# Seven block products in another order, with the sums between them, in a mixer kernel's channel stage

## Chip, cores and metric

The program runs on one core of a Trainium2 chip. The metric is device time in microseconds (us) of one execution; the time before is the median of three runs, 832.79 (832.41 to 833.27).

## What is computed

The reference is local attention (8 batches, 8 heads, 576 positions, 64 wide, a window of 64), whose output x (8 x 576 x 512) goes through a mixer:

```python
xt = x.transpose(0, 2, 1)
h = np.maximum(xt @ w_tok1, 0.0) @ w_tok2          # 576 -> 256 -> 576
u = x + h.transpose(0, 2, 1)
h2 = np.maximum(u @ w_ch1, 0.0) @ w_ch2            # 512 -> 1536 -> 512
return (u + h2).astype(np.float32)
```

The last two lines are the channel stage, which the change is about. All is float32. A product is made of three matmuls in the reduced format fp32r on values split in two: hi·hi, hi·lo and lo·hi, where hi is the value rounded by a copy and lo is what the copy left over.

## The kernel before

The program first does attention and the token mixing, and stores u to DRAM in nine chunks of 512 tokens. Then comes the channel stage: three **plain chunks** (numbers 0 to 2), each a first product (`gemm1`, twelve feature tiles `ft`) and a second one (`gemm2`, four output tiles `ct`, in two halves of six feature tiles each for chunks 1 and 2), and then three **pairs** of chunks, (3, 4), (5, 6) and (7, 8).

A pair uses the Winograd form of Strassen's scheme: the two chunks side by side are one matrix of 2 x 2 blocks, and a block product takes seven products, named m1 to m7, in place of eight. The sums of weight blocks that m5, m6, m7 and m3 need are made once, while the plain chunks run, by `weight_steps`: a generator of 24 steps for the first weight ("u") and 24 for the second ("d"), of which a plain chunk takes one or two behind each tile. A step adds weight blocks on VectorE (DVE), and `keep` splits the sum (ScalarE, ACT, copies hi; VectorE subtracts to lo) into buffers `whi` and `wlo`, three each, and stores both to DRAM (`w1s`, `w2s`) through SyncE's queue (SP). `load_unit` brings the weights of one pass back, three passes ahead.

The input sums of a pair (`sums`, `sum4`) and their splits (`prep`) are made beside the pair before, or beside chunk 2 for the first pair.

A pair runs three **groups** (`g`); a group is two **first products** (`first_product`, feature tiles 2g and 2g+1, here pass 1 and pass 2) and two **second products** (`second_product`, ct 0 and ct 1). Each of these four is 42 matmuls: seven products of two tiles of three matmuls. There are nine groups in all.

A first product writes four banks of PSUM, P, Q, R and S, a different four in pass 1 and pass 2, and the second products use the same two sets. m1 goes to P, m6 to Q, m7 to R, m5 to S (k < 4 starts a bank); m2, m3 and m4 are then added into P, S and R (`INTO`), so each of these three waits until the earlier content of its bank has been read. VectorE forms the chain (x1 is a copy of P by ScalarE, then x1 += Q, and so on) and, from the activated sums, the inputs of the second product: `raw_block` and `raw_low` are a block taken from a bank with ReLU and its lo part (VectorE), `sum_block` splits a sum t1 to t4 (hi on ScalarE, lo on GpSimd, POOL). Buffers of these have one copy each per pass.

A second product adds its banks into u2 and into the blocks c11, c12, c21, c22 of the output (`add`, tiles uf). In the last group of a pair (`final`), u2 is added into c12, c21 and c22, and the four blocks are stored. The hooks `last_first`, `last_second0` and `last_second1` put the splits for the next pair between the products of that group.

All engines work in the order in which the program is written here (the schedule is manual), each queue in order.

Of the kernel before, what the change touches and what calls it, by code (L numbers as in the profile page):

```python
# [34 lines left out]
CHUNK = 512  # L35
# [20 lines left out]
PRODUCTS = ("m1", "m6", "m7", "m5", "m2", "m3", "m4")  # L56
# [6 lines left out]
WW = 2 * P  # L63

# [22 lines left out]
def mixer_kernel(ctx: ExitStack, tc: tile.TileContext, qh, kh, vh, wt1, wt2, wc1, wc2, out):  # L87
# [472 lines left out]
    with ExitStack() as bctx:  # L560
# [146 lines left out]
        def weight_steps(name, whi, wlo, part, store, swap):  # L707

            for n in range(2 * NG):
# [17 lines left out]
                nc.vector.tensor_add(s1, s1, a)  # L727
# [3 lines left out]
                if swap:  # L731
                    nc.vector.tensor_sub(a, a, c)
                else:
                    nc.vector.tensor_sub(a, c, a)
                nc.vector.tensor_sub(c, s1, c)
# [45 lines left out]
        def prep(q, m, t, at=0, eng=nc.vector):  # L781
# [4 lines left out]
            split(nc.scalar, eng, c[:, 0, t], c[:, 1, t], raws[at][SOURCE[m]])  # L786
# [3 lines left out]
        for j in range(1, N_PLAIN):  # L790
# [4 lines left out]
            for half in range(2):  # L795
                g = []
                for ft in range(half * NH, (half + 1) * NH):
                    g.append(new_g(f"{j}_{ft}"))
                    gemm1(j, ft, u, g[-1])
                    for _ in range(2 if j == 1 and ft < 8 else 1):  # L800
                        next(steps, None)
# [31 lines left out]
                for ct in range(NCT):  # L833
# [3 lines left out]
                    next(steps, None)  # L837
# [24 lines left out]
        def first_product(n, q, f, after):  # L862
# [18 lines left out]
            def sum_block(m, x):  # L881
                split(nc.scalar, nc.gpsimd, *gc[m, i], x)

            x1, x2, g11, t1, t2, t3, t4 = (tmp("x1", 2), tmp("x2"), tmp("g11"), tmp("g12t"), tmp("g22t"),
                                           tmp("g3"), tmp("g4"))
            for k, m in enumerate(PRODUCTS):
# [7 lines left out]
                if m == "m1":  # L894
                    nc.scalar.copy(x1, pp)  # L895
                elif m == "m6":
                    nc.vector.tensor_add(x1, qq, x1)
                elif m == "m7":
                    nc.vector.tensor_add(x2, rr, x1)  # L899
                elif m == "m5":  # L900
                    nc.vector.tensor_add(qq, ss, x2)  # L901
# [167 lines left out]
```

## Time and profile before

| | |
|---|---|
| median of three runs | 832.79 us |
| the profiled execution | 831.14 us, its span 829.1 us |
| mean granted TensorE clock | 0.997 |
| busy: TensorE, VectorE, ScalarE, GpSimd | 800.3, 603.1, 389.4, 246.4 us |
| pair stage, first to last matmul | 457.05 to 825 us |

The span is what the profiler saw from the first to the last instruction; the profiled execution's own time holds some 2 us around it. A row of the timeline has the start, the length, the engine, the line, the operation, out<-in and, in brackets, how long the engine stood idle before it and what ended that. A row of the stretches has, behind the stretch and its length, the busy time of PE, PEld (weight loads), DVE, ACT and POOL with the number of instructions of each, the granted clock, the DMA share and GB/s. A row of the waits has who waited for whom, the total in us, how often, and the longest. A group's row has the busy time and the mean length of one in ns, then the idle time ahead. Names are the program's with buffer numbers left out: `gp` are the banks of a first product, `op` those of a second, x are x1 and x2, g, g12t and g22t the sums t1 to t4.

### The profile page before, as it was taken

Reading aid. Unit: us, or ns where it says so; the run is one execution under the profiler, and the core shown is the slowest. Engines: PE = TensorE matmul, PEld = TensorE weight load, DVE = VectorE, ACT = ScalarE, POOL = GpSimd, SP = SyncE. Lnnn points to the kernel's source line nnn. Section 1 sums busy time; section 2 is a strip of 40 time slices with the busy share of each in tenths; the row PEclk is TensorE's granted clock in tenths of the full one; section 3 lists DMA queues with packets and bytes.
Section 4 is the critical chain, followed back from the end, with each engine's and each line's share of the span. In section 5 each row is a group of like instructions: output and inputs, shape, how many; then the busy total and the mean of one; then the engine's idle time right before and its main releaser. Section 6 shows DMA issues by size and latency. Waiting matters only on the chain. (4 is left out here: it accounts for less than half of the span.)

```text
span 829.1 us, 15813 instructions
## 1 busy us (share of the span) xinstructions
PE 800.3 (97%) x5749; PEld 654.7 (79%) x5749; DVE 603.1 (73%) x1545; ACT 389.4 (47%) x1124; POOL 246.4 (30%) x225
## 2 busy tenths in 40 slices
PE   8989999999999999999999899999999999999997
PEld 6668888888888878788888677777777877787876
DVE  5978889799773993776858665658766669756566
ACT  7988988988964521232423322244323144324140
POOL 3632544444330000000000122639222648222231
PEclk9999999999999999999999999999999999999999
DMA  9837769677644629956537775755864746855532
GB/s 356 288 140 242 249 233 295 244 225 275 199 130 155 192 78 271 288 176 198 178 113 243 274 286 188 276 182 183 319 234 177 279 179 232 324 185 184 202 141 102
DMA packets 86829, 180.60 MB, mean 218 GB/s; under 512 B 8800, under 2 KB 51808, under 8 KB 84832
## 3 DMA queue, kind: packets, MB, share of 16 engines
q1 hardware_dynamic: 84640, 177.76, 62.3%
q10 hardware_dynamic: 2112, 1.84, 0.7%
q8 instruction: 45, 0.74, 0.4%
q14 instruction: 32, 0.26, 0.1%
HBM read 137.69 MB, written 41.88 MB: 217 GB/s over the span
## 5 line engine op out<-in xcount | busy, mean ns | idle before, releaser
L892 PE MATMUL gp<-m,w1hi 128*128 128x512 f32 x504 | 158.4, 396 | 8.8 <-DVE gp L901 5.6
L108 POOL TENSOR_TENSOR m5lo<-g12t,m5hi 128x512 fp32r<-128x512 f32 x18 | 23.4, 1299 | 418.9 <-ACT m5hi L105 418.9
L892 PEld LDWEIGHTS gp<-m,w1hi 128*128 128x128 f32 x504 | 94.0, 189 | 34.4 <-DVE gp L901 9.4
L301 ACT ACTIVATE e<-e,nm 128x128 f32<-128x128 f32 x288 | 112.2, 397 | 5.9 <-DVE nm L293 5.7
L892 PE MATMUL gp<-m,w1lo 128*128 128x512 f32 x252 | 98.7, 392 | 0.0
L939 DVE TENSOR_TENSOR uf<-op,uf 128x512 f32<-128x512 f32 (+1 forms) x91 | 61.0, 681 | 43.6 <-PE op L949 42.9
L293 DVE CUSTOM_DVE_ANT_0 e<-s,mask 128x128 f32<-128x128 f32 x288 | 65.3, 285 | 9.9 <-PE s L278 9.9
L633 PE MATMUL gp<-ulo,w1hi 128*128 128x512 f32 x144 | 56.0, 389 | 0.0
L633 PE MATMUL gp<-uhi,w1hi 128*128 128x512 f32 x144 | 56.0, 389 | 0.0
L633 PE MATMUL gp<-uhi,w1lo 128*128 128x512 f32 x144 | 56.0, 389 | 0.0
L301 ACT ACTIVATION_READ_ACCUMULATOR e<-e,nm 128x1 f32 x288 | 56.0, 194 | 0.0
L892 PEld LDWEIGHTS gp<-m,w1lo 128*128 128x128 f32 x252 | 47.7, 189 | 10.3
L108 POOL TENSOR_TENSOR xlo<-x,xhi 128x512 fp32r<-128x512 f32 x32 | 41.6, 1301 | 43.5 <-ACT xhi L105 42.8
L641 PE MATMUL op<-ghi,w2hi 128*128 128x512 f32 x128 | 50.0, 390 | 1.0 <-ACT ghi L620 1.0
L641 PE MATMUL op<-glo,w2hi 128*128 128x512 f32 x128 | 50.2, 392 | 0.6 <-DVE glo L621 0.6
L641 PE MATMUL op<-ghi,w2lo 128*128 128x512 f32 x128 | 49.8, 389 | 0.0
L895 ACT COPY x<-gp 128x512 f32<-128x512 f32 x18 | 10.5, 584 | 83.4 <-PE gp L892 83.4
L217 POOL TENSOR_TENSOR w<-r,c 128x384 f32<-128x384 f32 (+1 forms) x28 | 27.6, 986 | 70.2 <-DVE r L215 67.8
L308 PE MATMUL pp<-ident,e 128*128 128x128 f32 x288 | 45.4, 282 | 1.6
L320 PEld LDWEIGHTS xp<-v,pt 128*64 128x64 f32 x1152 | 36.6, 138 | 12.9 <-ACT e L301 9.4
L278 PE MATMUL s<-k,q 64*64 64x128 f32 x1152 | 41.5, 276 | 2.5 <-DVE ri L332 0.9
L416 PE MATMUL up<-t2hi,hhi 128*128 128x320 f32 (+1 forms) x128 | 43.1, 337 | 0.6 <-ACT t2hi L105 0.6
(203 smaller groups left out, 2043.7 us busy)
## 6 DMA issues: line engine op xcount, KB each, us to landing
v<-vh SPq DMA_DIRECT2D x36, 512.0 KB, 4.1
w1hi<-w1s SPq DMA_DIRECT2D x18, 896.0 KB, 4.8
w1lo<-w1s SPq DMA_DIRECT2D x18, 896.0 KB, 6.5
w1hi<-w2s SPq DMA_DIRECT2D x18, 896.0 KB, 4.5
w1lo<-w2s SPq DMA_DIRECT2D x18, 896.0 KB, 6.3
raw<-wc SPq DMA_DIRECT2D x32, 384.0 KB, 4.7
q<-qh SPq DMA_DIRECT2D x36, 256.0 KB, 4.5
k<-kh SPq DMA_DIRECT2D x7, 1280.0 KB, 7.7
```

The costliest lines, as they stand in the source:

```text
L108: eng_lo.tensor_sub(lo, src, hi.bitcast(F32))
L217: (nc.vector if late else nc.gpsimd).tensor_add(w, rf, cf)
L278: nc.tensor.matmul(so, qt[r, j, half], kbs[b][r, n:n + 2, j], start=True, stop=True)
L293: nc.vector.tensor_tensor_reduce(out=e[:, h], in0=s[:, h], in1=mk, scale=-scale, scalar=MAX_F32, op0=ALU.add, op1=ALU.min, accum_out=nm[:, ...
L301: nc.scalar.activation(e[:, h], e[:, h], AF.Exp, bias=nm[:, g:g + 1], scale=-1.0, accum_out=sm[:, g:g + 1])
L308: nc.tensor.transpose(pp[:, h], e[:, h], ident)
L320: nc.tensor.matmul(xp[half * BLK:(half + 1) * BLK, h], pts[h % 2][:, h // 2, half * BLK:(half + 1) * BLK], vt[:, half, h], start=True, sto ...
L416: nc.tensor.matmul(up[:, :n], hx[:, cs], w[:, tt * S + s0:tt * S + s0 + n], start=False, stop=(k == 6), skip_group_check=True)
L633: nc.tensor.matmul(gp, w[:, w1_at(ft, ct)], x[:, ct], start=(k == 0), stop=(k == 3 * NCT - 1))
L641: nc.tensor.matmul(op, w[:, ct, ft], x[:, cols], start=(first and k == 0), stop=(last and k == 3 * len(gs) - 1), skip_group_check=not (fir ...
L892: nc.tensor.matmul(b[INTO[m]], w[:, at], c[:, h, t], start=(k < 4 and z == y == 0), stop=(z == 1 and y == 2), skip_group_check=True)
L939: nc.vector.tensor_add(x, y, x)
```

## The change

It puts the products in another order, in the first products and in the second ones, changes the chain of sums to fit, hands the end of a first product (`tail`: rr, t4 and the m2 and m4 blocks) to the caller, which runs it between the next product's sums (or right behind, after pass 2), takes the weight steps by a table that ends in the first half of chunk 2, lets GpSimd add u2 into the output blocks except in the last pair, and splits the preparation for the next pair into its ScalarE and its GpSimd part. To fit the other signs of the chain, two weight sums of "d" are negated in the same instruction (`negate` in place of `swap`).

```diff
-PRODUCTS = ("m1", "m6", "m7", "m5", "m2", "m3", "m4")
+PRODUCTS = ("m1", "m6", "m5", "m7", "m3", "m2", "m4")
+STEPS_FT = {1: (2, 2, 2, 2, 1, 0, 2, 2, 0, 1, 1, 0), 2: (2, 0, 0, 2, 1, 0, 0, 0, 0, 0, 0, 0)}
+STEPS_CT = {1: (2, 2), 2: (3, 0)}
...
-                    for _ in range(2 if j == 1 and ft < 8 else 1):
+                    for _ in range(STEPS_FT[j][ft]):
                         next(steps, None)
...
-                    next(steps, None)
+                    for _ in range(STEPS_CT[j][half]):
+                        next(steps, None)
...
+            def tail():
+                nc.vector.tensor_add(rr, rr, x1)
+                raw_block("m2", rr)
+                yield
+                positive(t4, rr, t2)
+                sum_block("m4", t4)
+                yield
+                raw_low("m2", rr)
+                yield
...
                 if m == "m1":
                     nc.scalar.copy(x1, pp)
+                    next(earlier, None)
                 elif m == "m6":
                     nc.vector.tensor_add(x1, qq, x1)
+                    next(earlier, None)
+                elif m == "m5":
+                    nc.vector.tensor_add(x2, ss, x1)
+                    next(earlier, None)
                 elif m == "m7":
-                    nc.vector.tensor_add(x2, rr, x1)
-                elif m == "m5":
-                    nc.vector.tensor_add(qq, ss, x2)
+                    nc.vector.tensor_add(qq, rr, x2)
                     raw_block("m3", qq)
-                    raw_low("m3", qq)
-                elif m == "m2":
-                    nc.scalar.activation(g11, pp, AF.Relu)
-                    raw_block("m1", pp)
-                    raw_low("m1", pp)
                 elif m == "m3":
                     nc.vector.tensor_add(ss, ss, x1)
-                    positive(t1, ss, g11)
+                    nc.scalar.activation(g12, ss, AF.Relu)
+                    raw_low("m3", qq)
+                    positive(t3, qq, g12)
+                    sum_block("m7", t3)
+                elif m == "m2":
+                    positive(t1, pp, g12)
                     sum_block("m5", t1)
-                    positive(t2, qq, t1)
+                    nc.vector.scalar_tensor_tensor(out=t2, in0=qq, scalar=0.0, in1=t1, op0=ALU.max, op1=ALU.add)
+                    raw_block("m1", pp)
                     sum_block("m6", t2)
-                    positive(t3, pp, t2)
-                    sum_block("m7", t3)
-                else:
-                    nc.vector.tensor_add(rr, rr, x1)
-                    raw_block("m2", rr)
-                    positive(t4, rr, t2)
-                    raw_low("m2", rr)
-                    sum_block("m4", t4)
+                    raw_low("m1", pp)
...
-        ORDER2 = (("m1", 0), ("m1", 1), ("m6", 0), ("m7", 0), ("m5", 0), ("m5", 1), ("m6", 1), ("m7", 1),
+        ORDER2 = (("m6", 0), ("m7", 0), ("m5", 0), ("m1", 0), ("m1", 1), ("m7", 1), ("m5", 1), ("m6", 1),
                   ("m2", 0), ("m2", 1), ("m3", 0), ("m3", 1), ("m4", 0), ("m4", 1))
...
+            eng2 = nc.vector if q == len(pairs) - 1 else nc.gpsimd
...
-                    if m == "m4" and i == 1:
-                        add(c21[:, cols], bank[:, cols])
...
-                elif m == "m5":
+                elif m in ("m7", "m5"):
                     add(c22, bank)
                 elif m == "m6":
                     add(u2, bank)
                     if final:
-                        add(c22, u2)
-                elif m == "m7":
-                    add(c22, bank)
-                    store(3, c22)
-                    if final:
-                        add(c12, u2)
-                        add(c21, u2)
+                        add(c12, u2, eng2)
+                        add(c21, u2, eng2)
+                        add(c22, u2, eng2)
+                        store(3, c22)
...
             def last_second1(m):
-                if m == "m1":
+                if m == "m5":
                     for t in range(2):
-                        sum4(t, nc.gpsimd)
-                if m in ("m6", "m7"):
+                        sum4(t)
+                if m in ("m1", "m2", "m3"):
                     for t in range(2):
-                        prep(q + 1, {"m6": "m3", "m7": "m4"}[m], t, t)
+                        prep(q + 1, {"m1": "m3", "m2": "m2", "m3": "m4"}[m], t, t, part=0)
+                if m == "m4":
+                    for k in ("m3", "m2", "m4"):
+                        for t in range(2):
+                            prep(q + 1, k, t, t, nc.gpsimd, part=1)
```

On VectorE, between pass 1 and pass 2 of a pair's second group (numbers `_0_2` and `_0_3`: pair 0, feature tiles 2 and 3; `gp0_2_2` is bank R of pass 1), there stood before:

```order
L860 SCALAR_TENSOR_TENSOR g3_0_2_6715<-gp0_2_0_6692,g22t_0_2_6714 128x512
L917 TENSOR_TENSOR gp0_2_2_6694<-gp0_2_2_6694,x1_0_2_6710 128x512
L860 SCALAR_TENSOR_TENSOR g4_0_2_6716<-gp0_2_2_6694,g22t_0_2_6714 128x512
L860 SCALAR_TENSOR_TENSOR m2lo_0_2_6705<-gp0_2_2_6694,m2hi_0_2_6704 128x512
L897 TENSOR_TENSOR x1_0_3_6804<-gp0_3_1_6787,x1_0_3_6804 128x512
L899 TENSOR_TENSOR x2_0_3_6805<-gp0_3_2_6788,x1_0_3_6804 128x512
L901 TENSOR_TENSOR gp0_3_1_6787<-gp0_3_3_6789,x2_0_3_6805 128x512
L860 SCALAR_TENSOR_TENSOR m3lo_0_3_6801<-gp0_3_1_6787,m3hi_0_3_6800 128x512
```

And at the same place now (x2 now reads `gp0_3_3`, bank S):

```order
L871 SCALAR_TENSOR_TENSOR m1lo_0_2_6697<-gp0_2_0_6692,m1hi_0_2_6696 128x512
L899 TENSOR_TENSOR gp0_2_2_6694<-gp0_2_2_6694,x1_0_2_6710 128x512
L920 TENSOR_TENSOR x1_0_3_6798<-gp0_3_1_6781,x1_0_3_6798 128x512
L871 SCALAR_TENSOR_TENSOR t4g_0_2_6716<-gp0_2_2_6694,t2g_0_2_6714 128x512
L923 TENSOR_TENSOR x2_0_3_6799<-gp0_3_3_6783,x1_0_3_6798 128x512
L871 SCALAR_TENSOR_TENSOR m2lo_0_2_6707<-gp0_2_2_6694,m2hi_0_2_6706 128x512
L926 TENSOR_TENSOR gp0_3_1_6781<-gp0_3_2_6782,x2_0_3_6799 128x512
L929 TENSOR_TENSOR gp0_3_3_6783<-gp0_3_3_6783,x1_0_3_6798 128x512
```

The end of pass 1 (rr, t4, m2lo), which stood ahead of pass 2's x1 in one piece, now stands between pass 2's sums.

On GpSimd, at the end of the first pair (`m5_1` is the next pair's input of m5, `uf4` is c12 and c22, `uf3` is c21), there stood before, behind the lo parts of pass 2:

```order
L108 TENSOR_TENSOR m4lo_0_5_7127<-g4_0_5_7134,m4hi_0_5_7126 128x512
L108 TENSOR_TENSOR m7_1_7225<-r12_1_0_6882,m7_1_7225 128x512
L108 TENSOR_TENSOR m7_1_7225<-r12_1_1_6892,m7_1_7225 128x512
L108 TENSOR_TENSOR m5_1_7248<-t1_1_0_6888,m5_1_7248 128x512
L108 TENSOR_TENSOR m5_1_7248<-t1_1_1_6898,m5_1_7248 128x512
L108 TENSOR_TENSOR m2_1_7260<-r21_1_0_6886,m2_1_7260 128x512
L108 TENSOR_TENSOR m2_1_7260<-r21_1_1_6896,m2_1_7260 128x512
L777 TENSOR_TENSOR r11_1_0_6880<-r21_1_0_6886,t2_1_0_6889 128x512
L777 TENSOR_TENSOR r11_1_1_6890<-r21_1_1_6896,t2_1_1_6899 128x512
```

And now:

```order
L112 TENSOR_TENSOR m4lo_0_5_7121<-t4g_0_5_7128,m4hi_0_5_7120 128x512
L796 TENSOR_TENSOR m5_1_7238<-t1_1_0_6888,m5_1_7238 128x512
L796 TENSOR_TENSOR m5_1_7238<-t1_1_1_6898,m5_1_7238 128x512
L959 TENSOR_TENSOR uf4_6480<-u2_0_0_6388,uf4_6480 128x512
L959 TENSOR_TENSOR uf3_6478<-u2_0_0_6388,uf3_6478 128x512
L959 TENSOR_TENSOR uf4_6480<-u2_0_0_6388,uf4_6480 128x512
L796 TENSOR_TENSOR m7_1_7263<-r12_1_0_6882,m7_1_7263 128x512
L796 TENSOR_TENSOR m7_1_7263<-r12_1_1_6892,m7_1_7263 128x512
L959 TENSOR_TENSOR uf4_6480<-u2_0_1_6389,uf4_6480 128x512
L959 TENSOR_TENSOR uf3_6478<-u2_0_1_6389,uf3_6478 128x512
L959 TENSOR_TENSOR uf4_6480<-u2_0_1_6389,uf4_6480 128x512
L796 TENSOR_TENSOR m3_1_7306<-r22_1_0_6884,m3_1_7306 128x512
```

Six additions have come in, `sum4` (r11) has gone to VectorE, and six lo parts (m3, m2 and m4, of which the last row is the first) now stand behind all of them, where there were m2's two ahead of `sum4`.

On VectorE, at the end of chunk 1's first feature half (`glo1_5` is the lo part of the sixth feature tile), there stood before:

```order
L621 SCALAR_TENSOR_TENSOR glo1_4_5256<-gp1_4_5257,ghi1_4_5255 128x512
L715 TENSOR_TENSOR wau_2_5272<-w1hi_66,w1lo_67 128x256
L715 TENSOR_TENSOR wsu_2_5274<-w1hi_66,w1lo_67 128x256
L727 TENSOR_TENSOR wsu_2_5274<-wsu_2_5274,wau_2_5272 128x256
L715 TENSOR_TENSOR wbu_2_5277<-w1hi_66,w1lo_67 128x256
L108 TENSOR_TENSOR ulo_m5_2_5280<-wsu_2_5274,uhi_m5_2_5279 128x256
L621 SCALAR_TENSOR_TENSOR glo1_5_5287<-gp1_5_5288,ghi1_5_5286 128x512
```

And now:

```order
L625 SCALAR_TENSOR_TENSOR glo1_4_5256<-gp1_4_5257,ghi1_4_5255 128x512
L719 TENSOR_TENSOR wau_2_5272<-w1hi_66,w1lo_67 128x256
L719 TENSOR_TENSOR wsu_2_5274<-w1hi_66,w1lo_67 128x256
L625 SCALAR_TENSOR_TENSOR glo1_5_5278<-gp1_5_5279,ghi1_5_5277 128x512
L650 TENSOR_TENSOR uf1_4675<-op1_0_0_5295,uf1_4675 128x512
```

One sum step in place of two stands between the two lo parts, and the other one now comes behind the first output tile's addition.

More of the change, by code (lines that the diff above doesn't have):

```diff
@@ L785, in prep @@
             c = comb[q, m]
[L786 removed]
+            if part != 1:
+                nc.scalar.copy(c[:, 0, t], raws[at][SOURCE[m]])
+            if part != 0:
+                eng.tensor_sub(c[:, 1, t], raws[at][SOURCE[m]], c[:, 0, t].bitcast(F32))
         steps = all_steps()
@@ L980, in second_product @@
                     store(1, c12)
+                else:
+                    for cols in parts:
+                        add(c21[:, cols], bank[:, cols])
+                        if final:
+                            nc.sync.dma_start(out[pairs[q][0], :, ct + 2, cols], c21[:, cols])
                 after(m)
@@ L1020, in mixer_kernel @@
                     n += 1
+                for _ in tail:
+                    pass
                 if more and g == 1:
```

41 lines of the change are left out of this document (22 added, 19 removed).

## The prediction

> **What bounds the kernel now.** I read the page's first part, then busy time by stretch, then who TensorE (PE) waited for in the last 45% of the program, then the rows around those waits.
>
> ```profile
> PE 800.3 (97%) x5749; PEld 654.7 (79%) x5749; DVE 603.1 (73%) x1545; ACT 389.4 (47%) x1124; POOL 246.4 (30%) x225
> ...
> 400.00:457.00 57.00, 56.59 (x248) 46.19 (x247) 42.98 (x88) 18.64 (x39) 0.00 (x0) 1.00 0.52 176
> 457.00:501.60 44.60, 40.81 (x170) 32.60 (x170) 27.12 (x44) 12.66 (x23) 10.10 (x8) 0.96 0.68 256
> 501.60:541.60 40.00, 39.09 (x171) 31.31 (x170) 25.41 (x39) 10.48 (x18) 17.79 (x14) 1.00 0.65 236
> 541.60:583.60 42.00, 39.54 (x170) 31.12 (x169) 32.64 (x46) 17.96 (x32) 26.92 (x20) 1.00 0.59 207
> ```
>
> TensorE is the bound: 97% busy, all but full just ahead of the pair stage. The pair stage runs nine equal groups of 168 matmuls; the first takes 44.6 us, the second 40.0, the last of a pair 42.0. What would it take without waits? Two starts of undisturbed products, 42 matmuls apart, give the pace, and the first and last matmul give the stage:
>
> ```profile
> 541.37 0.61 PE L892 MATMUL gp<-m,w1hi 128*128 128x512 f32 x2
> 550.89 0.61 PE L892 MATMUL gp<-m,w1hi 128*128 128x512 f32 x2
> ...
> 457.05 0.61 PE L892 MATMUL gp<-m,w1hi 128*128 128x512 f32 x2
> 824.98 0.28 PE L949 MATMUL op<-m4hi,w1lo 128*128 128x256 f32 x1
> ```
>
> Pace: 9.52/42 = 0.2267 us. A product (six matmuls) is 1.36 us, a pass 9.52, a group 38.08, nine groups 342.7. The stage lasts 825.26 − 457.05 = 368.2 us, so 25.5 us are lost in it. That is all that this change can win there. To whom:
>
> ```profile
> PE gp L892 <- DVE gp L901: 5.6, 9, 0.7
> PE op L949 <- DVE uf L939: 3.6, 5, 1.1
> PE gp L892 <- ACT x L895: 3.3, 1, 3.3
> PE op L949 <- POOL m7lo L108: 2.2, 9, 0.3
> ```
>
> The waits shown add to 14.7 us; the other 10.8 lie in what each wait brings along (a matmul's modelled end overlaps its successor, and matmuls just behind a wait are slow). Four kinds of wait, then: once per group for VectorE (L901), once per group for GpSimd's m7lo, five times for the closing additions, once for ScalarE in the first group.
>
> **The change, part by part.**
>
> *Weight sums packed earlier.* ScalarE, in order, has the last weight sum ahead of x1, and that sum waits for a buffer whose store lands late:
>
> ```profile
> 452.12 12.49 DMA w2s<-dhi_m
> ...
> 464.99 0.40 ACT L105 CAST dhi_m<-wdd 128x256 fp32r<-128x256 f32 x1 [6.39 <-DMA w2s<-dhi_m]
> 465.30 0.58 ACT L895 COPY x<-gp 128x512 f32<-128x512 f32 x1
> ...
> 465.93 1.22 PE L892 MATMUL gp<-m,w1hi 128*128 128x512 f32 x2 [3.27 <-ACT x L895]
> ```
>
> The new table ends all sums within the second plain chunk's first half, over 20 us ahead of this. Nothing but TensorE's m1 is then ahead of x1: the first group falls to the others' length, 44.6 − 40.0 = 4.6 us.
>
> In the plain chunks the sums move as well:
>
> ```profile
> PE op L641 <- ACT ghi L620: 1.0, 1, 1.0
> PE op L641 <- DVE glo L621: 0.6, 3, 0.2
> ...
> 393.76 1.88 SPq L764 DMA_DIRECT2D r<-u_dram  x4
> ...
> 398.87 0.69 DVE L770 TENSOR_TENSOR t<-r,r 128x512 f32<-128x512 f32 x1
> ```
>
> The 1.0 us wait, with one of the three of 0.2 behind it, stood where two sum steps preceded the last feature tile's split; now one is in front of it, the one without a split: about 1.4 us back with the slow matmuls behind. Against it, in the next chunk: SyncE's load of r now stands behind one more step's stores, some 1.4 us later; VectorE's sums wait for it, and splits stand behind them: I take 0.7 us more wait there, bounded by 0 and 2.8, twice the slip. The last wait of 0.2 (0.5 with what it brings along) goes with the sums that stood ahead of it. Net gain 1.2, from −1 to 2.
>
> ```profile
> L727 DVE TENSOR_TENSOR wsd<-wsd,wad x6: 415/416/418, 383.4 to 449.7; 128x256 f32<-128x256 f32 x6
> ```
>
> Four steps are 12 VectorE operations of 0.42 us, 5.4 with their handovers. The second chunk's first half now holds three such rounds in its four output tiles: 16.2 us, and four additions of 0.69, beside 16.3 us of TensorE. VectorE gets behind by some 8 us, since each tile's steps start only when its addition can. The next half hides that: its first four feature tiles have a bank each, 4 × 12 matmuls = 10.9 us.
>
> *The order of the products.* Durations (mean ns):
>
> ```profile
> L860 DVE SCALAR_TENSOR_TENSOR m1lo<-gp,m1hi 128x512 fp32r<-128x512 f32 x18 | 12.5, 692 | 6.9 <-ACT m1hi L876 6.9
> L876 ACT ACTIVATE m1hi<-gp 128x512 fp32r<-128x512 f32 x18 | 10.8, 599 | 0.0
> L105 ACT CAST m5hi<-g12t 128x512 fp32r<-128x512 f32 x18 | 11.2, 622 | 38.7 <-DVE g12t L860 38.7
> L108 POOL TENSOR_TENSOR m5lo<-g12t,m5hi 128x512 fp32r<-128x512 f32 x18 | 23.4, 1299 | 418.9 <-ACT m5hi L105 418.9
> ...
> 554.57 0.69 DVE L860 SCALAR_TENSOR_TENSOR g<-gp,g22t 128x512 f32<-128x512 f32 x1 [0.73 <-ACT m2hi L876]
> 555.18 0.68 DVE L860 SCALAR_TENSOR_TENSOR m2lo<-gp,m2hi 128x512 fp32r<-128x512 f32 x1
> 556.44 0.69 DVE L897 TENSOR_TENSOR x<-gp,x 128x512 f32<-128x512 f32 x1 [0.58 <-ACT x L895]
> 557.23 0.69 DVE L899 TENSOR_TENSOR x<-gp,x 128x512 f32<-128x512 f32 x1
> 558.03 0.70 DVE L901 TENSOR_TENSOR gp<-gp,x 128x512 f32<-128x512 f32 x1
> 558.78 0.73 PE L892 MATMUL gp<-m,w1hi 128*128 128x512 f32 x2 [0.67 <-DVE gp L901]
> ```
>
> VectorE does the first pass's whole tail before the second pass's x1; x1, x2 and their sum follow in a chain 0.8 us apart, and the product into bank S waits. The number of VectorE operations stays at 12 per pass (8.3 us of 9.52); only their places change. I walk the queues with: VectorE 0.69 (0.79 when it needs its predecessor, 0.61 to the next start when not), ScalarE 0.60, GpSimd 1.3 (1.25 from start to start, first row below), and 0.27 us from a product's end to VectorE (m6 ends at 541.37 + 2.72 = 544.09, its addition began at 544.36).
>
> ```profile
> 484.68 1.25 POOL m6lo L108
> ...
> 544.36 0.69 DVE L897 TENSOR_TENSOR x<-gp,x 128x512 f32<-128x512 f32 x1 [2.10 <-PE gp L892]
> ```
>
> Pass 1, from its first matmul: x1 2.99–3.68; x2, straight from bank S after m5, 4.35–5.04; bank S is wanted by m3 at 5.44. The sum qq 5.71–6.41, ss 7.07–7.76, ScalarE's g12 to 8.39, m3lo to 8.37, t3 8.42–9.11, t1 to 9.71, t2 to 10.50, m1lo (behind ScalarE's m1hi) to 11.58. Pass 2 begins at 9.52: rr of pass 1 11.50–12.19, x1 12.51–13.20, t4 13.12–13.81, x2 13.87–14.56, m3 wants S at 14.96. So the wait for S goes, with 0.40 us in hand. Pass 2 ends at 19.04; its m7lo is done at 20.7, m5lo 21.9, m6lo 23.2, m4lo 24.5. The new order of the second products wants m7lo at 22.67, m5lo at 23.35, m6lo at 24.03, m4lo at 28.1: all in time, m6lo by 0.86. m1's second half wants m1lo (21.10) at 21.99. Both once-per-group waits go, and nothing is late in their place.
>
> *Closing additions.* m7's and m5's banks are now read ahead of m6's, so m4 no longer waits for bank R behind u2 and c22: four waits at the ends of pairs and one at the program's end go. The three additions of u2 go to GpSimd (not in the last pair), where these rows price them:
>
> ```profile
> L939 DVE TENSOR_TENSOR uf<-u,uf 128x512 f32<-128x512 f32 x18 | 16.5, 945 | 0.2
> L939 DVE TENSOR_TENSOR uf<-op,uf 128x512 f32<-128x512 f32 x89 | 60.3, 687 | 42.9 <-PE op L949 42.2
> ```
>
> On VectorE they took 0.95 us, stretched beside GpSimd's work; on GpSimd I take m5lo's 1.3. If all 12 moved additions lay on the path, 12 × (1.30 − 0.69) = 7.3 us would be lost. For elementwise additions the Trainium skill (GPSIMD Engine Reference, Engine selection) advises VectorE, since GpSimd is about 2 times slower with two inputs. The trace agrees in the ratio, 1299 to 692 ns; by that advice the sum below would be some 17 us in place of 24.
>
> They do not lie on it, mostly. From the start of a pair's last group, GpSimd has m4lo done at 24.9, m5's two parts at 27.4, ct 0's three additions at 31.2, m7's parts at 33.8. VectorE's c12 then waits until 28.7 and c21 until 30.0, with only next tile's additions behind them, which TensorE wants read from 34 on. In ct 1 the additions run 36.3–40.05, and behind them the low halves of m3, m2, m4 for the next pair: 41.3, 42.6, 43.8, 45.1, 46.4, 47.6. The next pair, from 38.08, wants them at 43.75, 44.43, 45.1, 45.8, 46.5 and 47.15: the last is 0.5 us late. Bounds: 0, if sum4 on VectorE is earlier, and 1.6 where GpSimd's start slips by a microsecond. SyncE holds c22's store until GpSimd is done, and the next unit's load behind it: 3 us later at most, for a unit wanted 16 us on.
>
> *End.* Bank R is now added after both halves of the last product, as one dependence: the last addition ends 0.4 us later behind the last matmul than before, where
>
> ```profile
> 825.29 0.42 DVE L939 TENSOR_TENSOR uf<-op,uf 128x256 f32<-128x256 f32 x1 [0.71 <-PE op L949]
> ```
>
> ended 3.4 us ahead of the span's end, in which the store lands.
>
> *Sum.* Of 25.5 us lost I leave 1.0 for the two pair ends and 1.3 for what I can't place (0.15 a group): 23.2. Plus 1.2 in the plain chunks, less 0.4 at the end: 24.0. The profiled execution took 831.14 (span 829.1 and 2.0 around it): 807.1. The median of the runs shown, 832.79, lies 1.65 above: 808.8.
>
> **The rivals.**
>
> *VectorE still the bound.* 12 operations a pass leave it 1.2 us of 9.52; if handovers cost 0.1 more each, S is late again and half of the nine-fold waits stay. Those are worth about 1.2 (L901) + 0.5 (m7lo) a group: half of 9 × 1.7 is 7.7 us: 816.5. For it: in hand are only 0.40 us. Against: the walk's latencies are those of the rows. Chance 0.10.
>
> *GpSimd the wait at pair ends.* Its in-order queue is the longest there: if the additions' 7.3 us show in full, as 3.6 us of late low halves at each of two ends, 816.1; if half, 812.5. For it: 0.5 us late by the walk already. The advice of the Trainium skill, above, speaks for this rival. Chance 0.10.
>
> *The packing does not do what it says.* If stores that land late (12.49 above) hold the packed steps, the backlog outgrows the 10.9 us, and the plain chunks lose 3 to 5 us: 812 to 814. Chance 0.09.
>
> *Slower than before.* t4 and m2lo of pass 1 now stand between x1 and x2 of pass 2. t4's one buffer is read by GpSimd's m4lo; if t4 waits, x2 waits, and S with it, in nine passes. Each microsecond beyond 0.40 costs 9; the 24 us are gone at 3.1 us of lateness, and 4 us give 9 × 3.6 − 24 = 8 over the old time: 841. Against it: that buffer's last reader is done at 24.5 of the group before, 26 us ahead of t4 at 13.12. Chance 0.04.
>
> **How the numbers follow.** My forecast, 808.8, has 0.67; its own range is 805.5 (every wait gone: 25.5 + 2.0 − 0.4 won, 805.7) to 812.5. Half of the gain lost in several ways at once still is faster. The range of 8 in 10 reaches to 816 for two of the rivals. 0.2% is about what a measurement of this kernel can tell from no change (1.7 us; the three runs spread 0.9). Faster 0.95, the same 0.01, slower 0.04.
>
> **What would show it.** Right: no wait of TensorE on x1's copy in the first group, no row of the S wait, none on m7lo, groups of 38.1 to 38.6 us, VectorE's x2 ahead of m7's end. GpSimd's low halves of m4 as the only wait at a pair's start, under 1.6 us. Wrong: waits on x2 or t4 in second passes (first rival, or the last), on GpSimd rows over 2 us (the second), on glo in the plain chunks over 3 us (the third).

## The result

The changed kernel takes 810.60 us (median of four runs, 810.35 to 812.39), where the kernel before took 832.71 beside it (832.41 to 833.27): a ratio of 0.9738, 95% interval 0.9721 to 0.9755. The profiled execution took 810.41 us, its span 808.4. Of the ten executions of one of the experiments (the packing alone, below) one took 1304.12 us at a granted clock of 0.557; the range and the ratio given for that kernel are those of the nine others.

First a line of the page's first part, then busy time in two stretches of about a group, then who TensorE waited for from 281 us on, all of the changed kernel:

```profile
PE 791.7 (98%) x5749; PEld 655.7 (81%) x5749; DVE 584.1 (72%) x1529; ACT 388.5 (48%) x1124; POOL 263.5 (33%) x241
...
458.00:496.00 38.00, 38.00 (x169) 31.35 (x168) 23.70 (x36) 11.43 (x20) 10.21 (x8) 1.00 0.61 233
...
573.00:611.00 38.00, 37.74 (x166) 30.75 (x166) 23.75 (x37) 11.53 (x20) 19.65 (x16) 1.00 0.83 308
...
PE op L645 <- ACT ghi L624: 1.5, 2, 1.0
PE op L645 <- DVE glox L625: 1.0, 1, 1.0
PE gp L914 <- POOL m L796: 0.5, 2, 0.3
PE op L645 <- DVE glo L625: 0.2, 1, 0.2
```

In the pair stage all four kinds of wait that the prediction named are gone. TensorE is full in it (38.00 of 38) but for the start of the second and third pair (37.74 and 37.80 of 38), where it waits for GpSimd's low halves. The waits that are left stand in the plain chunks (L645). The starts of the stages, from the changed kernel's timeline:

```profile
388.78 0.39 PE L637 MATMUL gp<-uhi,w1hi 128*128 128x512 f32 x1
405.10 0.39 PE L645 MATMUL op<-ghi,w2hi 128*128 128x512 f32 x1
...
458.45 0.62 PE L914 MATMUL gp<-m,w1hi 128*128 128x512 f32 x2
803.28 0.28 PE L970 MATMUL op<-m4hi,w1lo 128*128 128x256 f32 x1
```

These rows are the start of chunk 2, the start of its first half's second product, and the pair stage's first and last matmul. With the second products of chunk 0 (289.36) and chunk 2's second half (425.81), and the same places of the kernel before (289.45, 390.72, 407.04, 423.89, 457.05, 824.98), the difference of the profiled executions comes out:

| stretch | before | after | won |
|---|---|---|---|
| chunk 0's second products to chunk 2 | 101.27 | 99.42 | 1.85 |
| chunk 2, first half (two products of 72 matmuls) | 33.17 | 37.03 | −3.86 |
| chunk 2, second half | 33.16 | 32.64 | 0.52 |
| pair stage, to the end of the last matmul | 368.21 | 345.11 | 23.10 |
| last matmul to the end of the span | 3.84 | 4.84 | −1.00 |

That is 20.6 us, and the profiled times differ by 831.14 − 810.41 = 20.7. The pair stage won what was forecast. Chunk 2's first half lost far more: its 144 matmuls are 32.64 us at the pace, so the kernel before lost 0.5 us there and the changed one 4.4. This is the place in the changed kernel's timeline:

```profile
398.91 0.69 DVE L777 TENSOR_TENSOR t<-r,r 128x512 f32<-128x512 f32 x1 [2.46 <-DMA r<-u_dram]
...
408.43 0.50 PE L645 MATMUL op<-ghi,w2hi 128*128 128x512 f32 x1 [0.45 <-ACT ghi L624]
...
409.97 0.40 ACT L109 CAST dhi_m<-wdd 128x256 fp32r<-128x256 f32 x1 [1.60 <-DVE wdd L747]
410.28 0.59 ACT L624 ACTIVATE ghi<-gp 128x512 fp32r<-128x512 f32 x1
410.92 0.69 PE L645 MATMUL op<-ghi,w2hi 128*128 128x512 f32 x1 [1.04 <-ACT ghi L624]
411.65 0.79 PE L645 MATMUL op<-glo,w2hi 128*128 128x512 f32 x1
412.24 0.63 PE L645 MATMUL op<-ghi,w2lo 128*128 128x512 f32 x1
412.67 0.63 PE L645 MATMUL op<-ghi,w2hi 128*128 128x512 f32 x1
...
414.89 0.40 PE L645 MATMUL op<-ghi,w2hi 128*128 128x512 f32 x1
```

Two things are to be seen. ScalarE's high half at 410.28 stands behind a weight step's copy (409.97), and that one waits for VectorE's sum: the step holds the split, and the split TensorE. And from 411.65 on no releaser is named, yet from 412.24 on the matmuls come 0.43 us apart in place of 0.2267. By the pace, the 17th matmul of this product was due at 405.10 + 16 × 0.2267 = 408.73 and came at 411.65, 2.92 late; the 25th was due at 410.54 and came at 414.89, 4.35 late. So 2.9 us are waits and 1.4 are matmuls at a lower clock.

### The profile page after: what moved, and what is told of

Its sections match the earlier page's. It is cut to its first block, busy times and chain, and to the rows that moved or that the text cites. A ratio compares the mean times of both kernels' runs of the same rounds, so it can differ in the third digit from the quotient of the medians.

```text
span 808.4 us, 15812 instructions
## 1 busy us (share of the span) xinstructions
PE 791.7 (98%) x5749; PEld 655.7 (81%) x5749; DVE 584.1 (72%) x1529; ACT 388.5 (48%) x1124; POOL 263.5 (33%) x241
## 5 line engine op out<-in xcount | busy, mean ns | idle before, releaser
L914 PE MATMUL gp<-m,w1hi 128*128 128x512 f32 x504 | 155.8, 390 | 0.5 <-POOL m L796 0.5
L112 POOL TENSOR_TENSOR m7lo<-t3g,m7hi 128x512 fp32r<-128x512 f32 x18 | 23.3, 1296 | 363.4 <-ACT m7hi L109 363.4
L645 PE MATMUL op<-ghi,w2hi 128*128 128x512 f32 x128 | 50.7, 396 | 1.5 <-ACT ghi L624 1.5
L645 PE MATMUL op<-glo,w2hi 128*128 128x512 f32 x128 | 50.7, 396 | 0.3 <-DVE glo L625 0.2
L645 PE MATMUL op<-ghi,w2lo 128*128 128x512 f32 x128 | 50.3, 393 | 0.0
```

The lines of the kernel that those rows point to most:

```text
L112: eng_lo.tensor_sub(lo, src, hi.bitcast(F32))
L645: nc.tensor.matmul(op, w[:, ct, ft], x[:, cols], start=(first and k == 0), stop=(last and k == 3 * len(gs) - 1), skip_group_check=not (fir ...
L914: nc.tensor.matmul(b[INTO[m]], w[:, at], c[:, h, t], start=(k < 4 and z == y == 0), stop=(z == 1 and y == 2), skip_group_check=True)
```

## The experiments

All kernels are edits of the changed one, but for the packing alone, which is an edit of the one before. The time ahead of chunk 0's second products varies between executions. In seven of the twelve profiled ones these products began at 289.1 to 290.1 us. In the other five (tail_inline, one_last_piece, steps_after_sums, steps_in_load_wait, packing_alone) they began at 291.5 to 292.5, and in just these five TensorE's granted clock was low at 51 to 55 us (0.57 to 0.71, where the seven have 1.00). So beside each median stands the stretch from there to the end of the last matmul, of one execution. The changed kernel, load_early and one_last_piece, which lose the same in chunk 2, agree in it within 0.4 us. Medians of different rows agree less well, since the kernel before had medians of 830.79 to 832.71 beside them; differences of under 2 us are read from the stretch and the rows of the trace.

| kernel | median (range), us | ratio to before, 95% interval | stretch, us |
|---|---|---|---|
| before | 832.71 (832.41–833.27) | | 535.8 |
| changed kernel | 810.60 (810.35–812.39) | 0.9738 (0.9721–0.9755) | 514.2 |
| steps_late | 807.77 (807.47–810.40) | 0.9724 (0.9706–0.9741) | 511.2 |
| load_early | 810.40 (809.93–811.11) | 0.9749 (0.9734–0.9763) | 514.3 |
| steps_in_load_wait | 811.31 (809.19–812.66) | 0.9755 (0.9734–0.9777) | 513.8 |
| steps_after_sums | 807.81 (807.02–809.14) | 0.9716 (0.9691–0.9741) | 510.3 |
| packing_alone | 828.38 (827.50–830.87) | 0.9965 (0.9951–0.9979) | 532.3 |
| tail_inline | 823.68 (823.35–825.54) | 0.9907 (0.9890–0.9923) | 526.9 |
| m1_first | 822.77 (822.52–824.20) | 0.9898 (0.9874–0.9922) | 526.0 |
| adds_on_vector | 812.32 (811.56–812.64) | 0.9768 (0.9745–0.9791) | 515.6 |
| one_last_piece | 811.14 (809.44–812.11) | 0.9748 (0.9718–0.9777) | 513.9 |
| both_mended | 806.52 (806.21–810.59) | 0.9712 (0.9689–0.9735) | 510.1 |

### Where chunk 2 loses time: the place of the steps

The three steps behind the fourth and fifth product of chunk 2 go behind the seventh to ninth.

```diff
-STEPS_FT = {..., 2: (2, 0, 0, 2, 1, 0, 0, 0, 0, 0, 0, 0)}
+STEPS_FT = {..., 2: (2, 0, 0, 0, 0, 0, 1, 1, 1, 0, 0, 0)}
```

> The changed kernel with the three weight steps behind feature tiles 9 and 10 of ... that is, behind the fourth and fifth feature tile of chunk 2, moved behind tiles 6, 7 and 8 (one each). The changed kernel loses 4.3 us to TensorE waits at the start of chunk 2's first output tiles. Theory A, the steps between the splits: all of it goes, about 806.5 us. Theory B, the late load of the first raw blocks alone: 2 us or more of the wait stay, 808.5 us or more. Theory C, each alone is enough to uncover it and neither does without the other: as A here.

Measured (steps_late): 807.77, between A's 806.5 and B's 808.5, so the rows decide. Two stretches of the changed kernel and then the same two of this one (the third number from the end is the granted clock):

```profile
408.00:412.00 4.00, 2.28 (x5) 1.02 (x6) 2.91 (x6) 1.27 (x3) 0.00 (x0) 0.88 0.62 209
412.00:415.00 3.00, 3.00 (x9) 2.33 (x9) 2.06 (x5) 0.20 (x1) 0.00 (x0) 0.59 0.04 13
```

```profile
408.00:412.00 4.00, 4.00 (x19) 3.33 (x18) 2.45 (x6) 0.69 (x2) 0.00 (x0) 1.00 0.08 26
412.00:415.00 3.00, 3.00 (x15) 2.49 (x14) 2.36 (x7) 0.94 (x3) 0.00 (x0) 1.00 0.69 230
...
398.81 0.69 DVE L777 TENSOR_TENSOR t<-r,r 128x512 f32<-128x512 f32 x1 [2.39 <-DMA r<-u_dram]
```

Waits and low clock both go, and the first half takes 32.64 us, the pace. VectorE's wait for the load is still there (2.39 us), so the load alone does not stop TensorE: A or C holds, not B. Some 1.5 us were lost at 440 us instead (the second half takes 34.18 us, where the pace gives 32.64), where the steps now stand between other splits.

### The load, taken earlier

The first pair's first load is issued in chunk 1, behind the second output tile of its second half.

```diff
-            if last:
-                pools[0] = ...
-                load_raw(0, 0)
...
+                    if not last and half == 1 and ct == 1:
+                        pools[0] = ...
+                        load_raw(0, 0)
```

> The changed kernel with the first raw blocks' load (and its buffers) moved from chunk 2's start to behind the second output tile of chunk 1's second half; the weight steps stay where they are. Theory A, steps alone: VectorE's 2.5 us wait for the load goes, but TensorE's waits in chunk 2 stay at 2 us or more, 808.5 us or more. Theory B, load alone: they go, about 806.5 us. Theory C, both needed: they go here too, 806.5 to 807.

Measured (load_early): 810.40, no difference. The load's wait went, but another transfer's came, on ScalarE, and VectorE waited behind it:

```profile
390.56 0.41 ACT L109 CAST dhi_m<-wdd 128x256 fp32r<-128x256 f32 x1 [5.84 <-DMA w2s<-dhi_m]
```

A weight sum's buffer is free once its store has landed. The stores now stand behind the load on SyncE's queue, and those of dhi_m took longer to land (2.9 us in the median between 378 and 400 us, 1.7 in the changed kernel). VectorE began the input sums at 399.40, against 398.91, so this run does not tell what a load without a price would give.

### Steps into the time of the load's wait

```diff
-STEPS_FT = {..., 2: (2, 0, 0, 2, 1, 0, 0, 0, 0, 0, 0, 0)}
+STEPS_FT = {..., 2: (4, 0, 0, 0, 1, 0, 0, 0, 0, 0, 0, 0)}
```

> The changed kernel with two of chunk 2's early steps one stretch earlier: four behind its first product in place of two, none behind its fourth. VectorE then has them to do while it would stand 2.46 us for the loaded chunk (at 398.91 us in the changed kernel). Theory A (chunk 2's waits come from the sum of both, the idle time for the load and the steps between the splits, so either taken away is enough): the splits at 408.41 and 410.90 come about 2.4 us earlier, both waits and the slow matmuls behind them go, and the time is that of the steps placed late without their wait at 440: 806.3, within 805.8 to 807.3. Theory B (it is the steps' place between the splits, or their splits on ScalarE's queue, that holds the high halves, whenever VectorE is free): the step behind the fifth product still holds a high half, one wait of 0.5 to 1.2 us stays, and the time is 808.5 to 810.6.

Measured (steps_in_load_wait): 811.31, so my theory A fell; it lies over B's range too, but the stretch is the changed kernel's (513.8 for 514.2). The rows:

```profile
402.95 0.41 ACT L109 CAST dhi_m<-wbd 128x256 fp32r<-128x256 f32 x1 [2.46 <-DMA w2s<-dhi_m]
404.49 0.68 DVE L777 TENSOR_TENSOR t<-r,r 128x512 f32<-128x512 f32 x1
...
PE op L645 <- ACT ghi L624: 0.9, 1, 0.9
```

The steps did not fill the idle time: the copy of one of them waits 2.46 us for a store's landing, and the sums begin at 404.49. In the changed kernel, in load_early and here the time is lost to a transfer of this stretch, the load or a store, on whichever engine comes to it first. B was right that a step behind the fifth product still holds a high half (0.9 us), but chunk 2's first half loses as much as in the changed kernel, 4.4 us.

### The steps behind the input sums

```diff
-STEPS_FT = {..., 2: (2, 0, 0, 2, 1, 0, 0, 0, 0, 0, 0, 0)}
-STEPS_CT = {1: (2, 2), 2: (3, 0)}
+STEPS_FT = {..., 2: (1, 0, 0, 0, 0, 0, 0, 0, 0, 0, 0, 0)}
+STEPS_CT = {1: (2, 2), 2: (3, 1)}
```

> The 48 weight steps again, but none between the splits of chunk 2 except one at its start: the other three stand behind the first second products, and four in the last stretch of chunk 2, one behind each of its four additions, where VectorE in the changed kernel stands idle 1.6 to 3.4 us ahead of each. Theory A (the steps that stand between two splits held up the splits, and nothing else in chunk 2 did): both the 2.9 us of waits at 408 to 412 us and the 1.5 us that the later placing brought at 440 go, so 810.6 - 2.9 - (the slow matmuls behind them, about 1.5) = about 806.2, within 805.5 to 806.8, and no gap of TensorE over 0.3 us between 389 us and the pair stage. Theory B (VectorE has no room for the 48 steps in the plain chunks wherever they are put): a wait of 1 to 2 us turns up at the start of the pair stage or behind the sums of the first pair, and the time stays at 807.5 to 810.

Measured (steps_after_sums): 807.81, over A's bound and inside B's. The stretch shrank by 3.9 us, and chunk 2 has no wait left. B's wait came too, but small: 0.2 us for x2 in the first group (0.47 with what it brings along), since the last step's copy stands ahead of x1's and waits for a store:

```profile
459.96 0.41 ACT L109 CAST dhi_m<-wdd 128x256 fp32r<-128x256 f32 x1 [3.34 <-DMA w2s<-dhi_m]
...
PE gp L914 <- DVE x L923: 0.2, 1, 0.2
```

That is the first-group wait of the kernel before, in small.

### The packing alone

The kernel before, with the two tables of steps and nothing else of the change.

> The kernel before with the new table of weight steps and nothing else. If the first group's wait was the late weight sum: that wait of ScalarE's x1 goes (about 5 us with the slow matmuls), chunk 1's 1.7 us go, and chunk 2 loses 3 to 4 us more than before, so 828.5 to 830. If the first group waits for something else that the packing does not touch, the wait stays and chunk 2's loss makes it slower: 834 to 836. The S wait and the m7lo wait stay nine times each in both cases.

Measured (packing_alone): 828.38, just under the 828.5 of the first theory; the ratio of 0.9965 is 2.9 us of 832. TensorE's waits:

```profile
PE gp L896 <- DVE gp L905: 5.8, 9, 0.7
PE op L953 <- DVE uf L943: 3.7, 5, 1.1
PE op L644 <- ACT ghi L623: 1.3, 2, 1.0
```

The first group's wait on x1 is gone, the waits of the order stay (L905 and L943 here), and chunk 2's wait is there as in the changed kernel. The pair stage lasts 363.3 us, 4.9 less than before; the stretch from chunk 0's second products to it 169.0, 1.4 more than before's 167.6, against 1.5 more in the changed kernel. The first group takes 39.5 us, before 44.4. So the loss in the plain chunks is the packing's, and what all the rest of the change wins in the pair stage is 23.1 − 4.9 = 18.2 us.

### The end of pass 1 in one piece

The tail (rr, t4, m2 and m4 blocks) runs right behind its first product, ahead of the next one's sums.

```diff
+                    for _ in tail:
+                        pass
```

> The changed kernel with the end of each first product (rr, t4, m2 and m4 blocks) run right behind it, as before the change, in place of between the next product's sums. Theory: the shorter chain (x2 read straight from m5's bank, m5 ahead of m7) is what removes the wait for bank S; x2 of pass 2 then ends at 15.0 and S is wanted at 14.96, so 0.1 us a group: 810.6 to 812. Rival: the deferred end is what removes it; then 0.8 to 1.2 us come back in nine groups: 818 to 822.

Measured (tail_inline): 823.68, over the rival's range. I had held that the shorter chain is enough; by the stretch the deferral is worth 13 us. TensorE waits 10.2 us for x2, once in each of nine groups. The rows of one such place:

```profile
552.01 0.60 ACT L887 ACTIVATE m2hi<-gp 128x512 fp32r<-128x512 f32 x1 [0.86 <-DVE gp L899]
552.72 0.69 DVE L871 SCALAR_TENSOR_TENSOR t4g<-gp,t2g 128x512 f32<-128x512 f32 x1 [0.73 <-ACT m2hi L887]
553.44 0.62 ACT L109 CAST m4hi<-t4g 128x512 fp32r<-128x512 f32 x1 [0.83 <-DVE t4g L871]
553.97 0.58 ACT L917 COPY x<-gp 128x512 f32<-128x512 f32 x1
556.12 0.73 PE L914 MATMUL gp<-m,w1hi 128*128 128x512 f32 x2 [1.29 <-DVE x L923]
```

The handovers between ScalarE and VectorE come one after another: rr, m2hi, t4, m4hi, and only then, ScalarE being in order, the copy that x1 needs. In the changed kernel the copy stands ahead of m2hi, and x1 between rr and t4 fills one of those handovers.

### m1 first in the second products

```diff
-        ORDER2 = (("m6", 0), ("m7", 0), ("m5", 0), ("m1", 0), ("m1", 1), ("m7", 1), ("m5", 1), ("m6", 1),
+        ORDER2 = (("m1", 0), ("m1", 1), ("m6", 0), ("m7", 0), ("m5", 0), ("m7", 1), ("m5", 1), ("m6", 1),
```

> Only the order of the second products: m1's two halves ahead of m6, m7 and m5, as in the kernel before. Theory A (the sums of pass 2 end just ahead of their use, so the order in which the second products take them counts): in the changed kernel's trace the second products of a group begin at 553.85 us, m1's high half of pass 2 is written at 555.27 and its low half at 555.99; with m1 first the fourth matmul would be due at 554.5 and wait 0.9 us, the fifth another 0.5, so 1.4 us in each of nine groups, 12.6 us: 823, within 820 to 825. Theory B (the work on ScalarE and VectorE was shortened by the other changes so far that the order of the second products doesn't matter): 810.6, and at most 812.

Measured (m1_first): 822.77, 12.2 us more than the changed kernel, as A had it. A group's rows:

```profile
479.72 0.69 DVE L871 SCALAR_TENSOR_TENSOR m1lo<-gp,m1hi 128x512 fp32r<-128x512 f32 x1 [0.39 <-ACT m1hi L887]
479.74 0.49 PE L970 MATMUL op<-m1hi,w1hi 128*128 128x512 f32 x1 [0.63 <-ACT m1hi L887]
480.46 0.50 PE L970 MATMUL op<-m1lo,w1hi 128*128 128x512 f32 x1 [0.23 <-DVE m1lo L871]
```

TensorE comes to m1's second half just as it is made. A group takes 39.5 us in place of 38.2. The first halves of m6, m7 and m5, put ahead of m1, give 9 × 0.2267 = 2.0 us, more than the 1.3 that are lost without them.

### The closing additions on VectorE

```diff
-            eng2 = nc.vector if q == len(pairs) - 1 else nc.gpsimd
+            eng2 = nc.vector
```

> All closing additions on VectorE: twelve additions (two pair ends, six each) of 0.69 us there in place of 1.30 us on GpSimd. Theory A (they lie beside TensorE's work on either engine, and only the two 0.5 us waits of the first products for the low halves on GpSimd hang on them): those two waits go, 810.6 - 1.0 = 809.6, within 809.0 to 810.6. By the rule that GpSimd is about twice as slow (the Trainium skill, GPSIMD Engine Reference, Engine selection), if the additions stood on the path, 12 x 0.6 = 7.2 us would be won: 803.4. Theory B (VectorE is the bound at the pair ends, so that what GpSimd took from it was a gain): 12 x 0.6 = 7.2 us lost, 817.8, with waits for VectorE at the two pair ends.

Measured (adds_on_vector): 812.32, with intervals that overlap (the changed kernel's and this one's); the stretch says 1.4 us longer. The waits on GpSimd's low halves went, as A had it, but waits for VectorE's x2 took their place, as B had it, though with 2.4 us in all and not 7.2:

```profile
572.64 3.37 DVE L959 TENSOR_TENSOR uf<-u,uf 128x512 f32<-128x512 f32 x3
575.93 1.87 DVE L959 TENSOR_TENSOR uf<-op,uf 128x512 f32<-128x512 f32 x3
578.50 0.69 DVE L923 TENSOR_TENSOR x<-gp,x 128x512 f32<-128x512 f32 x1
579.34 0.70 PE L914 MATMUL gp<-m,w1hi 128*128 128x512 f32 x2 [1.18 <-DVE x L923]
```

Beside GpSimd's work the three additions took 3.37 us on VectorE, 1.12 each where 0.69 was taken; in the last pair, where GpSimd has nothing to do beside them, they took 1.89. GpSimd needs 3.8 for them. So 2 × 1.4 us come in and 2 × 0.5 go out: 1.8, near the 1.7 by which the pair stage is longer. The Trainium skill (GPSIMD Engine Reference, Engine selection) puts elementwise additions on VectorE, as GpSimd is about twice as slow with two inputs. The durations agree, 1.30 to 0.69 us; the 7.2 us that this would win if the additions lay on the path are not there, because most of them lie beside TensorE's work on either engine.

### The last product in one piece

```diff
-LAST_PARTS = 2
+LAST_PARTS = 1
```

> The last block product's last half as one piece of 512 columns in place of two of 256. The changed kernel adds both pieces only once the last matmul has ended (803.60, 0.76 us together), and sends two stores (0.84 us of issue). Theory A (the two pieces bring nothing in this order, and cost a second store): one addition of 0.69 us and one store of about 0.42 us of issue, so the stretch from the last matmul to the end goes from 4.84 to about 4.4 us, the time 810.2. Theory B (a store of half the size lands sooner by more than its issue costs): 0.3 to 0.6 us longer, 811.

Measured (one_last_piece): 811.14, no difference that the interval can tell. The end of the changed kernel, then of this one:

```profile
803.60 0.76 DVE L959 TENSOR_TENSOR uf<-op,uf 128x256 f32<-128x256 f32 x2 [0.26 <-PE op L970]
804.05 0.84 SPq L999 DMA_DIRECT2D out<-uf  x2
```

```profile
805.19 0.39 PE L970 MATMUL op<-m4hi,w1lo 128*128 128x512 f32 x1
806.34 0.33 SPq L999 DMA_DIRECT2D out<-uf  x1
```

From the last matmul's end (805.58) to the span's end (810.1) it is 4.5 us here and 4.84 in the changed kernel, each from one execution: near A's 4.4. Both pieces are added after the last matmul, so cutting in two gains nothing in this order.

### Both places mended

Steps as in steps_after_sums, but two behind chunk 2's first product, so that the last addition ahead of the pair stage has none behind it; and ct 0's closing additions on VectorE.

```diff
+STEPS_FT = {..., 2: (2, 0, 0, 0, 0, 0, 0, 0, 0, 0, 0, 0)}
+STEPS_CT = {1: (2, 2), 2: (3, 1)}
...
-            eng2 = nc.vector if q == len(pairs) - 1 else nc.gpsimd
+            eng2 = nc.vector if q == len(pairs) - 1 or ct == 0 else nc.gpsimd
```

> Two changes at once, as a possible better kernel: the steps as in the run that put them after the sums, but with two behind the first product and so none behind the last addition ahead of the pair stage (where a wait of 0.47 us for x2 had come); and the closing additions of ct 0 on VectorE, those of ct 1 on GpSimd. Theory A (each wait has the cause that its releaser names, and they add up): against the changed kernel's 5.65 us of gaps after 281 us some 1.8 stay (1.1 in chunk 0, 0.1 in each group), so the last matmul ends about 344.0 us behind the start of the pair stage in place of 344.8, and the time is 805.5, within 804.5 to 806.8. Theory B (VectorE is then too late at the pair ends, as with all closing additions on it): a wait of 0.5 to 1.3 us for x2 in two groups, 806.5 to 808.

Measured (both_mended): 806.52, the lowest median, though not to be told from the two other placements of the steps. It lies in the ranges of both theories, so the rows decide. All of its gain is chunk 2's; the half about the pair ends failed under both theories, as the wait on GpSimd stayed and none on x2 came:

```profile
566.80 3.80 POOL L959 TENSOR_TENSOR uf<-u,uf 128x512 f32<-128x512 f32 x3 [4.68 <-DMA out<-uf]
...
PE gp L914 <- POOL m L796: 0.5, 2, 0.2
```

With half of its additions gone GpSimd stands idle for 4.68 us, and ct 1's additions begin no sooner. They need ct 1's u2, which VectorE finishes at 566.72, 0.08 us ahead of them (the row names a store; in the changed kernel too they begin 0.09 us behind u2). The six low halves behind them end as late as before, and the 0.5 us stays. The pair stage takes 345.4 us (799.20 − 453.77), 0.3 more than in the changed kernel, where A had 0.8 less: its first group takes 38.45 us for 38.15, as a step's copy again waits for a store ahead of x1's.

## Why the prediction was right or wrong

**The pair stage: right, in size and in place.** 23.2 us were to be won, 23.1 were. VectorE's walk stands to within 0.1 us. The changed kernel's second products of one group begin at 553.85, so its pass 1 began 84 matmuls, 19.04 us, earlier, at 534.81:

```profile
546.38 0.69 DVE L899 TENSOR_TENSOR gp<-gp,x 128x512 f32<-128x512 f32 x1
547.32 0.69 DVE L920 TENSOR_TENSOR x<-gp,x 128x512 f32<-128x512 f32 x1 [0.24 <-PE gp L914]
547.92 0.68 DVE L871 SCALAR_TENSOR_TENSOR t4g<-gp,t2g 128x512 f32<-128x512 f32 x1
548.61 0.69 DVE L923 TENSOR_TENSOR x<-gp,x 128x512 f32<-128x512 f32 x1
...
553.85 0.39 PE L970 MATMUL op<-m6hi,w1hi 128*128 128x512 f32 x1
```

In the walk's time these are 11.57, 12.51, 13.11 and 13.80, where 11.50, 12.51, 13.12 and 13.87 were worked out; m3 wants bank S at 14.96, and x2 is done at 14.49. Its 0.40 us in hand were real, and tail_inline shows what they hang on: without the deferral the same chain is 1.3 us late. m1_first shows the like of the second products. Undoing either one costs 12 to 13 us; these are not shares of the 18.2, which is less than both together. What the five waits behind the closing additions were worth by themselves no run shows; their row had 3.6 us before, and they are gone.

GpSimd's part of the walk held less well. In this group, a pair's last, m6lo is done at 23.7 in place of 23.2, since splits for the next pair stand ahead of it; it is wanted at 24.03, so 0.3 us were in hand and not 0.86. The 0.15 us a group that the sum could not place are there too, 38.23 us from group to group where the pace gives 38.08. A part of them has a row: m2's second matmul comes 0.33 us behind its first (559.28 us), whose weights could be loaded only behind VectorE's addition to u2.

**The first group: right.** 4.6 us were given to the packing; packing_alone's pair stage is 4.9 shorter.

**GpSimd at the pair ends: right,** 0.5 us in each of two places (38.7 us for these groups in place of 38.2; the wait itself is 0.25 by its row), and in the place named (the last low half of m4).

**The plain chunks: the term that was mis-sized.** +1.2 was forecast, −1.5 came. Its first part, chunk 1's wait, held: 1.6 us of the 1.85 up to chunk 2 lie in chunk 1 (65.49 us, before 67.06). Its last part held too: 0.5 in chunk 2's second half. The failed step is the middle one, 0.7 us more wait in chunk 2's first half with a bound of 2.8: it was 3.9. I had worked out the load's slip (1.4 us against the chunk's start, 1.8 by the rows) and let VectorE's sums slip with it, and the sums did: they begin at 398.91, before at 398.87, in a chunk that starts 1.94 us sooner. But I priced the slip by itself. It reaches the splits behind together with the three steps that now stand behind the fourth and fifth product, where the kernel before had two; and the slow matmuls, for which my bound had nothing, add 1.4. So chunk 1's gain was given back at once: TensorE came 1.9 us sooner to work that the transfers still held at the old time. steps_late and steps_after_sums show that moving the steps alone takes all of it back; load_early and steps_in_load_wait show that giving VectorE the load or the work at another time does not, since a store's landing then holds ScalarE, and VectorE behind it. Whether a load that cost the stores nothing would do it as well stays open. The rival on the packing had named 3 to 5 us lost in the plain chunks, by late stores and a backlog. Its sign was right, but not its mechanism: in the changed kernel's chunk 2 the only transfer that is waited for is the load, and the second half, which the backlog was to reach, has no wait.

**The end: mis-sized.** 0.4 us were to be lost, 1.0 were. one_last_piece accounts for 0.3 of the 0.6 that I missed, the second store and its addition; what the other 0.3 is stays open.

**From the profiled execution to the median.** The sum gave 807.1 for the profiled execution, which took 810.41: 3.3 us off, 2.7 of it in the plain chunks and 0.6 at the end. The median, 810.60, is only 1.8 above the 808.8, because the 1.65 us that were added for the kernel before are 0.2 here. That nearness is luck.

## What to carry to other kernels

When a wait is taken out upstream, the work downstream comes due that much sooner: check each later product against the times at which its inputs are really held (a load, a store's buffer), which need not move with it. Small work packed between the splits of a product holds them on two in-order engines at once, and is better put where the product behind needs nothing made. The same work on VectorE in another order, between the next step's sums and not ahead of them, was worth 13 us here without one operation saved.

## What the hardware showed that I had not expected

TensorE's clock fell though no single wait was long. From 407.82 to 411.65 us of the changed kernel it lost time ahead of five matmuls, 1.2 us the most at once, 2.9 us of 3.8 in all. The granted clock was 0.50 from 411.07 to 414.48 us, with matmuls 0.427 us apart (412.67 to 413.95, three steps):

```profile
407.66:411.07 3.41, 1.70 (x6) 0.63 (x4) 2.69 (x7) 1.61 (x4) 0.00 (x0) 1.00 0.62 210
411.07:414.48 3.41, 3.37 (x8) 2.29 (x9) 2.06 (x5) 0.00 (x0) 0.00 (x0) 0.50 0.23 77
```

In all eight executions that lost over 4 us in chunk 2's first half the clock was low for 3.41 us, and in the 3.41 us ahead of that TensorE had stood idle for 1.4 to 1.7 us in several gaps. The same 3.41 us of low clock followed the single wait of 3.27 us in the first group of the kernel before. Cut into pieces of this length, with their edges on those of a low stretch, no execution has more than 1.3 us of idle time in any other whole piece between 281 us and its last matmul, and there the clock stayed full: in the groups of m1_first and tail_inline, at the pair ends of adds_on_vector, at 440 us in steps_late. What between 1.3 and 1.4 decides, or whether it is the sum at all, no run was made to show.

The Trainium skill (TensorE: Matmul & The Clock Gate, Part 1) gives half the clock after an idle window of about 3.4 us and 426.7 ns from start to start for 512 columns at that clock. The rows agree with the spacing; the piece ahead of the low clock was busy for half of its length here. The Trainium skill (TensorE: Matmul & The Clock Gate, Why this matters for your kernels) asks for no idle gap over about 3 us. Here several gaps, none over 1.2 us, came ahead of the low clock.
